# Two experts' weights loaded early into freed slots, four experts' weights behind the row fetch, and 22 extra products

## The chip, the cores and the metric

The kernel runs on one core of a Trainium2 chip. The core has TensorE (PE; matrix products), VectorE (DVE), ScalarE (ACT), GpSimd (POOL) and SyncE (SP), which here only issues transfers; 16 DMA engines move the data. The metric is the device time of one execution in microseconds; less is better.

## What is computed

An attention block (a recurrence with a decaying state, "RWKV-7") is followed by a mixture of experts that keeps at most 80 tokens for each expert:

```python
def _moe_ref(x, w_gate, w1, w2, capacity):
    logits = x @ w_gate                       # x: 3072 tokens x 320, 8 experts
    expert_idx = np.argmax(logits, axis=1)
    probs = softmax(logits)
    gate_w = probs[np.arange(N), expert_idx]
    out = np.zeros((N, D))
    for e in range(E):
        tok_idx = np.where(expert_idx == e)[0]
        if len(tok_idx) > capacity:           # 80: the largest gates stay
            gw = gate_w[tok_idx]
            tok_idx = tok_idx[np.argpartition(-gw, capacity)[:capacity]]
        h = np.maximum(x[tok_idx] @ w1[e], 0.0)          # 320 x 1024
        out[tok_idx] = gate_w[tok_idx, None] * (h @ w2[e])   # 1024 x 320
    return out
```

The attention has batch 4, 8 heads, 768 steps and head size 40; its output, one row of 320 for each of 3072 tokens, is x.

## The kernel before

The program has three parts.

**Part one, attention and gates.** 24 units (12 stretches of 64 steps, two pairs of batches) go through three nested helpers, `prepare`, `solve` and `finish`. The instructions aren't issued as written: each is handed with `add` to a planner (class `Plan`), with an engine, an estimated duration, the keys of the buffers that it reads and writes and a due time, and the planner writes out one list. Buffers are rings: `kb` (scaled k and b, ten slots of 4 KB per partition), `ah` (scaled a, ten slots of 2 KB) and `P` have a slot for each of the last ten units, `raww` two. All of them lie in the pool `hold`, which ends with part one. A unit's token rows go to the tensor `x_rows` in DRAM in batches (`rows_go`, L817; the last two batches are two units each). The gates are ranked as they come: `rank_early`, `rank_four`, `rank_late` and `rank_last` take the largest gates of each expert out in groups of eight (`extract`, L846 and L848, on VectorE) and merge sorted lists (`merge`, L853 and L865) into `tops[0]` and `tops[1]`. `rank_late` and `rank_last` use two `raww` slots, `pair_a` and `pair_b`, as scratch.

**Part two, the slots.** From `tops` comes a threshold for each expert (`thr`, `thw`, `thr_p`), then a 0/1 matrix `sel` of kept tokens (bf16, 128 x 384, called `selm` when flat), two products that count them (`tot` L1025, `pos` L1027), a scan, and the slot of each token. `hot` (three blocks of eight units, L1039) times `ids` gives `ids_p` (24 small products, L1042), and from it come the row numbers `idx_g` and `idx_s`. The order inside parts two and three is not written by hand: a scheduler of the framework sets it, engine by engine.

**Part three, the experts.** `load_expert` (L978 to L981) issues four transfers on SP for one expert: the first 256 rows of w1, the other 64 rows in two halves (`w1r`), and w2. All eight experts' weights have a place of their own in the pool `wpool`, which reuses the memory of `hold`, and all eight calls stand ahead of part two on SP. SP's transfers share eight completion semaphores, so that the ninth waits for the first. `gather(e)` (L1066, GpSimd) fetches the 80 rows of expert e from `x_rows` with an indirect DMA. `turn_x` transposes them (L1077, L1078) to `xe`; `first_layer` has 64 products with the 256 rows (L1092) and 32 with the rest (L1098); `second_layer` 80 products with w2 (L1111); `turn_y` transposes back, scales, and scatters the rows into the output (L1124, GpSimd).

## Time and profile before

| what | value |
|---|---|
| time, median of 3 runs | 559.41 us (554.07 to 560.3) |
| profiled execution | 556.64 us, of which the span is 554.9 us |
| PE busy in the span | 418.9 us (75%) |
| DVE busy | 311.2 us (56%) |
| POOL busy | 224.7 us (40%) |
| ACT busy | 182.0 us (33%) |
| moved by DMA | 73.06 MB, mean 132 GB/s |

The profile records one execution. Its span runs from the first to the last instruction; the profiled execution's own time is 1.7 us longer. Busy time is the sum of an engine's instructions; those that only issue a transfer or wait are not counted. A share of the whole span is a mean over three very different parts, so a table by stage is of more use here than the totals. [...]

### The profile page before, as it was taken

How to read it: one execution, taken by the hardware profiler on the slowest of the kernel's cores; microseconds unless marked ns; L12 is line 12 of the kernel's file. 1: busy time of each engine (PE TensorE's matmuls, PEld its weight loads, DVE VectorE, ACT ScalarE, POOL GpSimd, SP SyncE). 2: the span in 40 equal slices, each digit the busy share in tenths (PEclk: the TensorE clock that was granted, in tenths of full speed). 3: DMA queues.
4: the chain of work that ended last, by engine and by line, in shares of the span. 5: the costliest groups of instructions: out<-in, count | busy, mean ns of one | idle time of the engine just before them, and what ended most of it. 6: DMA issues, size and time to landing. Idle time of an engine off the chain costs nothing. (4 is left out here: it accounts for less than half of the span.)

```text
span 554.9 us, 24379 instructions
## 1 busy us (share of the span) xinstructions
PE 418.9 (75%) x10769; PEld 363.9 (66%) x10769; DVE 311.2 (56%) x706; ACT 182.0 (33%) x353; POOL 224.7 (40%) x395
## 2 busy tenths in 40 slices
PE   2754199797929988989898998999888102788795
PEld 2643078686818877878787887888777101677794
DVE  5868968536504745773577443966496995011121
ACT  2432063543522453444454443445223000110000
POOL 7010101888488410898599513883000002300111
PEclk9978569989866998988899799999699755688799
DMA  8775477576692677677577185314510009999900
GB/s 135 116 114 113 65 171 145 90 116 123 122 214 61 118 170 132 148 138 121 127 139 188 50 150 124 84 31 121 117 26 28 2 24 335 324 333 330 289 15 20
DMA packets 241453, 73.06 MB, mean 132 GB/s; under 512 B 217908, under 2 KB 235716, under 8 KB 241348
## 3 DMA queue, kind: packets, MB, share of 16 engines
q1 hardware_dynamic: 211428, 65.50, 52.3%
q10 hardware_dynamic: 29152, 4.36, 4.9%
q8 instruction: 85, 1.39, 1.0%
q0 software_dynamic: 768, 1.64, 1.0%
q14 instruction: 20, 0.16, 0.1%
HBM read 53.26 MB, written 18.13 MB: 129 GB/s over the span
## 5 line engine op out<-in xcount | busy, mean ns | idle before, releaser
L498 POOL TENSOR_TENSOR tmp<-lt 128x30 f32<-128x30 f32 (+9 forms) x150 | 86.1, 574 | 60.5 <-DMA lt<-blocks 49.7
L500 POOL TENSOR_TENSOR lt<-lt,tmp 128x30 f32<-128x30 f32 (+9 forms) x150 | 87.7, 585 | 11.8
L707 DVE TENSOR_TENSOR UL<-ps,mask 128x832 f32<-128x832 f32 x24 | 24.5, 1023 | 47.3 <-PE ps L702 47.3
L758 PE MATMUL ps<-wsel,xT 128*128 128x192 f32 x192 | 38.4, 344 | 2.3 <-DVE xT L748 1.4
L344 PE MATMUL ps<-ident,raww 128*128 128x128 f32 x88 | 17.5, 333 | 27.2 <-DMA raww<-in_w_dram 27.2
L344 PE MATMUL ps<-ident,kb 128*128 128x128 f32 x192 | 33.8, 304 | 4.8 <-DVE kb L407 3.5
L369 DVE TENSOR_TENSOR_SCAN P<-dec,begins 128x520 f32<-128x520 f32 x24 | 30.7, 1288 | 8.1 <-ACT dec L365 8.0
L485 POOL MEMSET nt<- 32x1024 f32 x12 | 11.4, 946 | 58.4 <-ACT nt L417 58.0
L758 PEld LDWEIGHTS ps<-wsel,xT 128*128 128x128 f32 x192 | 31.8, 196 | 4.4 <-DVE xT L748 1.7
L1124 POOL DMA_INDIRECT out_dram<-y,idx_s x8 | 7.4, 924 | 66.6 <-DVE y L1123 66.6
L735 DVE TENSOR_TENSOR st<-ps,st 128x832 f32<-128x832 f32 (+1 forms) x24 | 23.8, 991 | 18.6 <-PE ps L724 18.6
L377 DVE TENSOR_TENSOR_SCAN iv<-dec,ends 128x520 f32<-128x520 f32 x24 | 29.9, 1245 | 4.4 <-ACT ivc L396 3.7
L1111 PE MATMUL yp<-hT,w 128*64 128x80 f32 x640 | 29.6, 249 | 3.2 <-issue 3.0
L344 PEld LDWEIGHTS ps<-ident,raww 128*128 128x128 f32 x88 | 12.2, 169 | 28.8 <-DMA raww<-in_w_dram 22.8
L452 DVE TENSOR_TENSOR psi<-ps,mask 128x512 f32<-128x512 f32 x24 | 16.4, 688 | 25.4 <-PE ps L437 23.5
L407 DVE TENSOR_TENSOR kb<-rawkb,ps 128x640 f32<-128x640 f32 x22 | 17.9, 814 | 21.6 <-PE ps L344 13.2
L1111 PEld LDWEIGHTS yp<-hT,w 128*64 128x64 f32 x640 | 26.6, 148 | 5.0 <-issue 3.5
L344 PEld LDWEIGHTS ps<-ident,kb 128*128 128x128 f32 x192 | 23.7, 154 | 8.6 <-DVE kb L407 3.5
L611 ACT COPY rv<-ps 128x1024 f32<-128x1024 f32 x24 | 24.3, 1013 | 11.1 <-PE ps L344 7.2
L655 PE MATMUL ps<-VL,psi 64*64 64x104 f32 x768 | 27.2, 289 | 0.5 <-DVE VL L628 0.3
L1092 PE MATMUL hp<-xe,w 128*64 128x80 f32 x512 | 24.3, 259 | 2.8 <-issue 2.3
L1092 PEld LDWEIGHTS hp<-xe,w 128*64 128x64 f32 x512 | 23.1, 159 | 3.3 <-issue 2.4
(176 smaller groups left out, 953.7 us busy)
## 6 DMA issues: line engine op xcount, KB each, us to landing
w<-in_moe_w_dram SPq DMA_DIRECT2D x8, 1280.0 KB
w<-in_moe_w_dram SPq DMA_DIRECT2D x8, 1024.0 KB
VL<-in_v_dram SPq DMA_DIRECT2D x96, 40.0 KB, 2.3
out_dram<-zero SPq DMA_DIRECT2D x8, 480.0 KB
raww<-in_w_dram SPq DMA_DIRECT2D x44, 80.0 KB, 3.1
rawkb<-in_k_dram SPq DMA_DIRECT2D x44, 80.0 KB, 3.5
rawkb<-in_b_dram SPq DMA_DIRECT2D x44, 80.0 KB, 3.1
rawr<-in_r_dram ACTq DMA_DIRECT2D x84, 40.0 KB, 3.6
```

What stands on the lines that cost most here:

```text
L344: nc.tensor.matmul(o, lhsT=i, rhs=ident, start=True, stop=True, is_transpose=True, skip_group_check=True)
L369: nc.vector.tensor_tensor_scan(at("P", n), at("dec", n)[:, 0 : H * SEG], begins, 0.0, op0=Alu.mult, op1=Alu.add)
L377: nc.vector.tensor_tensor_scan(at("iv", n)[:, H * SEG : 0 : -1], at("dec", n)[:, H * SEG : 0 : -1], at("ends", n)[:, H * SEG : 0 : -1], 0. ...
L498: e.tensor_tensor(out=tv, in0=t3[:, 0:s, s : s + 1].to_broadcast([128, s, n]), in1=t3[:, s : s + 1, s + 1 :].to_broadcast([128, s, n]), op ...
L500: e.tensor_tensor(out=t3[:, 0:s, s + 1 :], in0=t3[:, 0:s, s + 1 :], in1=tv, op=Alu.add)
L611: nc.scalar.copy(at("rv", n).rearrange("p (k c) -> p k c", k=2), ps[:, bank(kr) : bank(kr) + 2, :])
L655: nc.tensor.matmul(ps[T * x : T * x + T, b0 + q, X * i : X * i + X], lhsT=psi[rows, q, i, :], rhs=at("VL", n)[rows, vo : vo + X], start=i ...
L707: nc.vector.tensor_tensor(out=view(at("UL", n), 0, (M4 * X, 2), (1, M4 * X)), in0=view(ps[:, bank(ku), :], 0, (512, 2), (1, M4 * X)), in1= ...
L735: nc.vector.tensor_tensor(out=view(st, o, (BS, M4), (step, 2), (1, n_)), in0=view(flat, 512 * bank(ky) + o, (4 * T, M4), (step, 2), (1, n_ ...
L758: nc.tensor.matmul(ps[:, b0, WS * m : WS * m + WX], lhsT=at("xT", n)[:, 2 * T * cof(m, 0) : 2 * T * cof(m, 0) + 2 * T], rhs=wsel_[:, WS * ...
L1092: nc.tensor.matmul(hp[j][c : c + 64, b // 2, :], lhsT=w1[:, i, FH * j + 64 * b : FH * j + 64 * b + 64], rhs=xe[:, i, :], start=i == 0 and ...
L1111: nc.tensor.matmul(yp[c : c + 64, b // 2, :], lhsT=w2[:, f, 64 * b : 64 * b + 64], rhs=hT[:, f, :], start=f == 0 and b < 2, stop=f >= (FK ...
```

## The change

**Early weights.** `early_weights(0)` and `early_weights(1)` are planned in part one. Each issues seven transfers on SP: w1 into two `kb` slots, w1's last 64 rows in two halves into an `ah` slot, and w2 in three pieces into three `kb` slots. Expert 0 takes the slots of units 14 to 18, expert 1 those of units 19 to 23. All ten `kb` slots, three `ah` slots and the scratch tiles `cd`, `la`, `lb` and `lc` move from `hold` to a pool `keep_` that stays until the end. `pair_a` and `pair_b` move from two `raww` slots to one of those `ah` slots.

**Later weights.** Only experts 2 to 7 have a place in `wpool`. Experts 2 and 3 are loaded where all were loaded; experts 4 to 7 are loaded behind `gather(0)` and a transfer of one word of its rows to DRAM (`word`) on SP, which waits for that gather to land.

**Products.** 22 products of `ones_b` with `selm` (bf16, 128 x 384) go into a PSUM tile `warm` that nothing reads.

```diff
+WARM = 22
...
+    KEPT = [("ah", NM - 10), ("ah", NM - 5), ("ah", NM - 8)] + [("kb", n) for n in range(LOOK)]
+    kept = {(n, i % LOOK): keep_.tile([128, COLS[n]], F32, name=f"{n}_{i % LOOK}") for n, i in KEPT}
...
-        buf = {n: [hold.tile([128, COLS[n]], F32, name=f"{n}_{i}") for i in range(RINGS[n])] for n in COLS}
+        buf = {n: [kept[n, i] if (n, i) in kept else hold.tile([128, COLS[n]], F32, name=f"{n}_{i}")
+                   for i in range(RINGS[n])] for n in COLS}
...
-        cd, la, lb, lc = (hold.tile([128, 128], F32, name=name) for name in ("cd", "la", "lb", "lc"))
+        cd, la, lb, lc = (keep_.tile([128, 128], F32, name=name) for name in ("cd", "la", "lb", "lc"))
...
-        pair_a, pair_b = at("raww", NM), at("raww", NM + 1)
+        pair_ = at("ah", NM - 8)
+        pair_a, pair_b = pair_[:, 0:256], pair_[:, 256:512]
...
+        def early_weights(e):
+            ks = range(NM - 10 + 5 * e, NM - 5 + 5 * e)
+            kbs = [at("kb", n) for n in ks]
+            rest = at("ah", ks[0])
+            w2s = [kbs[2 + i][:, 0 : DM * c].rearrange("p (c d) -> p c d", d=DM) for i, c in enumerate((3, 3, 2))]
+            weights[e] = kbs[0:2], rest, [w2s[f // 3][:, f % 3, :] for f in range(FK)]
+
+            def go():
+                for i in range(2):
+                    nc.sync.dma_start(kbs[i], moe_w1[e, 128 * i : 128 * i + 128, :])
+                for j in range(2):
+                    nc.sync.dma_start(rest[64 * j : 64 * j + 64], moe_w1[e, KW:, FH * j : FH * j + FH])
+                for i, o in enumerate(w2s):
+                    c = o.shape[1]
+                    nc.sync.dma_start(o, moe_w2[e, 384 * i : 384 * i + 128 * c, :].rearrange("(c p) d -> p c d", p=128))
+            add("SP", 4.5, 2.0, 0.0, go, [("tops", 0)],
+                [("kb", n) for n in ks] + [("ah", ks[0])], dma=7.5)
+
+        for e in range(2):
+            early_weights(e)
         rank_late()
         rank_last()
...
-    for e in range(E):
+    AHEAD = 4
+    for e in range(2, AHEAD):
         load_expert(e)
...
+        warm = ps_l.tile([128, NSEL], F32, name="warm")
+        for i in range(WARM):
+            nc.tensor.matmul(warm, lhsT=ones_b, rhs=selm, start=True, stop=True)
         row = sl.tile([cap, E], F32, name="row")
...
-    for e in range(E):
+    gather(0)
+    word = nc.dram_tensor("word", (1, 1), F32, kind="Internal")
+    nc.sync.dma_start(word[:, :], rows[0][0:1, 0:1])
+    for e in range(1, E):
         gather(e)
+    for e in range(AHEAD, E):
+        load_expert(e)
```

In part one the built order of every engine stays as it was, but for the early transfers on SP and the place of one merge of `rank_late` among the last VectorE rows. On SP, at the end of part one, there stands before (`lb<-la` is a merge's transfer, `w` and `w1r` are weights, one row for each call):

```order
L870 DMA lb<-la 8x128
L817 DMA x_rows<-xg_139 128x2x321 x2
L978 DMA w_0_6995<-in_moe_w_dram 128x2x1024
L980 DMA w1r_6996<-in_moe_w_dram 64x512 x2
L981 DMA w_0_6997<-in_moe_w_dram 128x8x320
L978 DMA w_1_7002<-in_moe_w_dram 128x2x1024
```

The two last writes of `x_rows` stand in a row there, and the weights of all experts follow. At the same place there stands now, with expert 0's weights in `kb` and `ah`:

```order
L879 DMA lb<-la 8x128
L824 DMA x_rows<-xg_142 128x2x321
L975 DMA kb_83<-in_moe_w_dram 128x1024
L975 DMA kb_84<-in_moe_w_dram 128x1024
L977 DMA ah_76<-in_moe_w_dram 64x512 x2
L980 DMA kb_85<-in_moe_w_dram 128x3x320
L980 DMA kb_86<-in_moe_w_dram 128x3x320
L980 DMA kb_87<-in_moe_w_dram 128x2x320
```

Expert 0's and expert 1's transfers went between the two writes of `x_rows`. Further on in SP's rows, from expert 1's last piece to expert 4's first:

```order
L980 DMA kb_82<-in_moe_w_dram 128x2x320
L824 DMA x_rows<-xg_142 128x2x321
L1004 DMA w_2_7012<-in_moe_w_dram 128x2x1024
L1006 DMA w1r_7013<-in_moe_w_dram 64x512 x2
L1007 DMA w_2_7014<-in_moe_w_dram 128x8x320
L1004 DMA w_3_7019<-in_moe_w_dram 128x2x1024
L1006 DMA w1r_7020<-in_moe_w_dram 64x512 x2
L1007 DMA w_3_7021<-in_moe_w_dram 128x8x320
L1160 DMA word<-rows 1x1
L1004 DMA w_4_7167<-in_moe_w_dram 128x2x1024
```

The last write of `x_rows` and experts 2 and 3 stand ahead of `word`, experts 4 to 7 behind it. On PE in part two there stands before:

```order
L1025 MATMUL tot<-sel,ones_b 128x384
L1027 LDWEIGHTS after_b
L1027 MATMUL pos<-sel,after_b 128x384
L1042 LDWEIGHTS hot
L1042 MATMUL ids_p<-ids,hot 80x24
```

There the products with `hot` follow `pos` at once. Now 13 of the 22 products stand between `pos` and the first product with `hot`, and three behind each eight of those; this is the end of the first eight and the first triple:

```order
L1069 LDWEIGHTS hot
L1069 MATMUL ids_p<-ids,hot 80x24
L1073 LDWEIGHTS ones_b
L1073 MATMUL warm<-sel,ones_b 128x384
L1073 LDWEIGHTS ones_b
L1073 MATMUL warm<-sel,ones_b 128x384
L1073 LDWEIGHTS ones_b
L1073 MATMUL warm<-sel,ones_b 128x384
L1069 LDWEIGHTS hot
L1069 MATMUL ids_p<-ids,hot 80x24
```

The scheduler spread the 22 products over part two; only the last three stand behind all the products that `idx_g` needs.

## Rows read from the trace of the kernel before

**Rows 1.** Busy time by stage: each engine, granted clock, DMA share, GB/s.

```profile
433.50:456.60 23.10, 0.61 (x3) 0.09 (x2) 21.88 (x98) 0.73 (x3) 0.56 (x3) 0.57 0.04 14
456.60:467.00 10.40, 3.16 (x27) 2.20 (x27) 7.85 (x17) 0.86 (x3) 0.90 (x4) 0.50 0.93 299
467.00:474.40 7.40, 0.00 (x0) 0.00 (x0) 0.00 (x0) 0.00 (x0) 5.38 (x8) 0.50 1.06 339
474.40:524.40 50.00, 41.93 (x859) 38.32 (x861) 8.51 (x20) 5.04 (x21) 5.41 (x6) 0.81 1.06 323
524.40:554.90 30.50, 23.71 (x609) 22.10 (x605) 5.61 (x12) 1.31 (x3) 4.58 (x5) 0.95 0.11 34
```

**Rows 2.** Timeline of SP's issues from 425 us: start, us, what.

```profile
428.05 17.90 SPq L817 DMA_DIRECT2D x_rows<-xg  x2
456.79 0.37 SPq L978 DMA_DIRECT2D w<-in_moe_w_dram  x1
```

**Rows 3.** Waits of SP's queue: total us, times, longest.

```profile
SPq L978 <- DVE tops L846: 8.3, 1, 8.3
```

**Rows 4.** Timeline, all engines, part two to the first layer of expert 0.

```profile
459.17 0.48 PE L1025 MATMUL tot<-sel,ones_b 128*128 128x384 bf16 x1 [0.99 <-DVE sel L1020]
459.44 0.53 PE L1027 MATMUL pos<-sel,after_b 128*128 128x384 bf16 x1
...
463.19 2.30 DVE L1039 TENSOR_TENSOR hot<-slot,iot 128x640 bf16<-128x640 f32 x3
...
464.07 2.18 PE L1042 MATMUL ids_p<-ids,hot 128*80 128x24 bf16 x24 [4.11 <-DVE hot L1039]
...
466.50 0.17 DVE L1046 TENSOR_SCALAR idx_g<-row 80x8 int32<-80x8 f32 x1
...
475.78 4.53 PE L1092 MATMUL hp<-xe,w 128*64 128x80 f32 x64 [0.50 <-DVE xe L1080]
...
480.25 1.27 PE L1098 MATMUL hp<-xe,w1r 64*64 64x80 f32 x32
```

**Rows 5.** Instructions on the tile rows: the gathers and all its transfers' landing.

```profile
L1066 POOL DMA_INDIRECT rows<-x_rows,idx_g x8: 906/910/1132, 468.0 to 476.7; - x8
...
DMA to landing us min/median/max: 6.4/6.9/8.0
```

**Rows 6.** Landing of the scatters into the output, from the tile view of out_dram.

```profile
DMA to landing us min/median/max: 2.4/3.0/7.1
```

**Rows 7.** Timeline of PE: the first products of experts 1 to 7's first layers.

```profile
482.54 0.28 PE L1092 MATMUL hp<-xe,w 128*64 128x80 f32 x1
...
488.32 0.23 PE L1092 MATMUL hp<-xe,w 128*64 128x80 f32 x1
...
499.42 0.23 PE L1092 MATMUL hp<-xe,w 128*64 128x80 f32 x1
...
511.32 2.43 PE L1092 MATMUL hp<-xe,w 128*64 128x80 f32 x64
...
524.42 0.34 PE L1092 MATMUL hp<-xe,w 128*64 128x80 f32 x1
...
532.84 0.23 PE L1092 MATMUL hp<-xe,w 128*64 128x80 f32 x1
...
540.30 0.23 PE L1092 MATMUL hp<-xe,w 128*64 128x80 f32 x1
...
542.74 0.78 PE L1098 MATMUL hp<-xe,w1r 64*64 64x80 f32 x32
```

**Rows 8.** PE alone in stretches of 1 us: busy, granted clock, DMA share, GB/s.

```profile
436.00:437.00 1.00, 0.00 (x0) 0.97 0.00 0
437.00:438.00 1.00, 0.00 (x0) 0.50 0.00 0
...
518.00:519.00 1.00, 0.00 (x0) 0.93 1.02 394
519.00:520.00 1.00, 0.38 (x7) 0.50 1.10 277
```

## The prediction

> **What bounds the kernel now.** I read the end of the program first, because everything the diff moves lies there. The table by stage [rows 1] cuts it into five. From 433.5 to 456.6 us VectorE alone works (21.88 of 23.10 us): it ranks the gates. The DMA engines are nearly free (share 0.04, 14 GB/s) and TensorE is busy for 0.61 us. From 456.6 to 467.0 the slots of the chosen tokens are worked out, a chain through VectorE and TensorE. From 467.0 to 474.4 no compute engine but GpSimd does anything: the rows of expert 0 are on their way. From 474.4 to 524.4 the DMA engines are full (1.06, 323 GB/s) and TensorE is busy for only 41.93 of 50.00 us. From 524.4 to the end TensorE sets the pace and the DMA share is 0.11.

> So the weights are the bound from 456.8 to about 525. SyncE issues the second-last write of x_rows at 428.05 and the last one 17.9 us later, and the first weight at 456.79 [rows 2]; before that weight it waited 8.3 us for VectorE's last MAX8 [rows 3], since the weight tiles take memory that the ranking still used. An expert has 320 x 1024 + 1024 x 320 words of 4 bytes, 2.62 MB; 8 of them are 21.0 MB, at 323 GB/s 65 us.

> What that costs TensorE is seen in the starts of the first layers for expert 0 and the others [rows 4, 7]: 475.78, 482.54, 488.32, 499.42, 511.32, 524.42, 532.84 and 540.30. The distances are 6.76, 5.78, 11.10, 11.90, 13.10, 8.42 and 7.46. The last has all weights present and no wait; the three of 11 to 13 are waits for weights.

> **The change part by part.**

> *Weights of experts 0 and 1.* Fourteen DMAs now stand on SP right behind the x_rows write of 428.05. The slots that they fill have no reader left after 433.5, when TensorE has three instructions in 23 us [rows 1]. 5.24 MB at 323 GB/s are 16.2 us, so they are done at about 446 to 450, in a stage where the DMA engines are free: cost nothing. Behind them on SP stands only the last x_rows write, issued at about 445.6 as before [rows 2] or up to 4 us later; it is needed by the fetch at 468.0 [rows 5], so it has some 15 us to spare. If that cover were gone, each us would be lost one for one.

> *Weights of experts 2 and 3.* The ranking's scratch moves into a slot that stays, so these no longer wait for the last MAX8 but for the last x_rows write, which I put at 449 (445.95 and about 3 us to land). 16.2 us more put their end at 465 to 468, before or just at the row fetch. Expert 2 is wanted some 20 us later.

> *Weights of experts 4 to 7 behind the row fetch.* SP waits for the first gather to land before it issues anything; queued behind it are only these 16 DMAs, and TensorE waits for them. They start at about 472 and need 10.5 MB / 323 GB/s = 32.5 us, to 505. By the starts worked out below expert 4 is wanted at 500 (its own weights land at about 481), expert 7 at 522. Cost nothing; the rate would have to fall under 10.5 MB / 50 us = 210 GB/s to matter, and the lowest full stage shows 299 [rows 1].

> *The row fetch.* A gather landed 6.4 us after its issue at the least while the weights ran [rows 5]. Scatters of as many rows landed in 7.1 at the most and 3.0 us in the median [rows 6], and five of the eight were issued after 524.4 [rows 1], when the weights had all but ended. With no weights on the engines I take 3.0: expert 0's rows at 471.0 instead of 474.4, **-3.4 us**. Bounds: 2.4, the least of the scatters (-4.0), and 6.4, nothing gained. [...]

> *TensorE without waits for weights.* From 475.78 to 540.30 are 64.52 us. With weights present I keep the first two distances (6.76 and 5.78, weights were there) and put 7.46 for the other five: 49.84. That is **-14.7 us**. The bound on the other side is 8.42, the other distance with its weights landed early in it, for all five: 54.64, so -9.9. I take 7.46, because it is the only one without a stretch at the lower clock. The part after the last start, 540.30 to 554.9, stays.

> *The 22 products.* In the built order they don't stand where the source has them: 13 come between pos and the first product for ids, three behind each group of eight. [...] I take **+0.8 us**, since which level holds there is open. Upper bound: 0.48 us each, the duration of tot, one after another: 13 end at 466.2, 2.1 late, and 6 more cost 2.9: +5.0. Lower bound: at the upper level the last eight products need only half their time behind the third hot (465.49), -0.4.

> *The clock at the first layer.* Expert 0's first layer took 475.78 to 481.52, 5.74 us, at the lower level; expert 7's took 540.30 to 543.52, 3.22 us [rows 4, 7]. If the products held the clock up until the rows land, 2.5 us would be saved. But the last products end at about 467 and the rows come at 471. In an idle stretch of the kernel before, from 433.5, the granted clock is 0.97 at 436 to 437 and 0.50 after; in a later one it is 0.93 at 518 to 519, with no product running, and 0.50 in the next [rows 8]. So I take **0**, with -2.5 as the bound.

> Sum: -3.4 - 14.7 + 0.8 = **-17.3 us**. The profiled execution took 556.64 us (span 554.9), so 539.3; it stands 2.8 us under the median of the three runs, 559.41, and on that median I forecast **542 us**.

> **The rivals.**

> *The clock stays up.* Then another 2.5 us are gained: 539.6. For it: the gap between the last product and the rows is only some 4 us. Against it: both idle stretches of rows 8 end at 0.50. [...]

> *The fetch is no shorter.* If its 6.4 us are its own and not the weights', term one goes and 545.5 is left. Against it: the scatters' 3.0.

> *The late weights bind.* Experts 4 to 7 start 15 us later than DMA engines allow. If the rate falls to 180 GB/s, expert 7 lands at 530 instead of the wanted 522: 550. No stage of rows 1 with full queues shows that.

> *The change doesn't take hold.* If the early DMAs were held until 456.8 as now, the first four experts would land at 491, the last four, behind the gather, at 525 as now, and the time would be 556 to 560. Against it: nothing between 428 and 456 in their slots is still read.

> *Slower.* TensorE becomes the only bound, so its clock decides. At the lower level a cycle is 5.74 / 3.22 = 1.78 times as long, so each us of the stage spent there costs 0.44 us; after 39 us of the some 64 the gain of 17.3 is spent, and with all of it the time is about 587. For it: in the stage 474.4 to 524.4 the mean granted clock is 0.81. Against it: that stage has idle stretches, and from 524.4 on, with none until the end, it is 0.95 [rows 1].

> **How the numbers follow.** Chances: the forecast 0.72, the clock stays up 0.10, the fetch no shorter 0.10, late weights 0.02, no hold 0.03, slower 0.03. Low end: 559.4 - 4.0 - 14.7 - 0.4 - 2.5 = 537.8, and since the runs of before reach 5.3 us below their median, 535. High end: with one term at its bad bound the time is 545.5 (fetch), 546.9 (cycles of 8.42) or 546.3 (products); with two of them up to 551. I set 549. A measurement of this kernel tells about 1% (5.6 us) from no change; the three runs spread by 1.1%. Faster by more than that are the first four, 0.94; within it the fifth, 0.03; slower 0.03.

> **What would show it.** In the changed profile: weights of experts 0 and 1 issued at 428 to 442 and a DMA share near 1 there; expert 2's first weight issued at about 449; the first gather landing about 3 us after issue; the first layer of expert 0 at 472 to 473; distances of about 7.5 us from expert 2 on and no wait of TensorE for weights; the first products for ids at 464 and the last at about 467; the clock at 0.50 when expert 0 starts. I'd be wrong if the distances stay at 8 us or more with weights present, if idx_g comes several us later, or if the stretch before 456 grows while 10 MB of weights are written beside the ranking.

## The result, and the profile after

The changed kernel took **540.48 us** in the median (538.6 to 543.25, 4 runs) and the kernel before 557.94 (554.07 to 560.3, 4 runs): a ratio of 0.970, 95% interval 0.962 to 0.977. The forecast was 542.0 us. The profiled execution took 539.98 us with a span of 538.2. The number was met; the way to it was not, as the rows show.

The table by stage of the changed kernel, with the stages of [rows 1] (columns: stretch, its length, busy time of PE, PEld, DVE, ACT and POOL, TensorE's granted clock as a share of full speed, DMA share, GB/s; in both kernels' traces the clock is at each moment 1.00 or 0.50, so a value between is a stretch with both):

```profile
428.00:450.90 22.90, 0.59 (x2) 0.09 (x2) 21.68 (x97) 1.40 (x6) 1.43 (x7) 0.57 0.93 291
450.90:460.90 10.00, 7.86 (x49) 4.24 (x49) 7.49 (x16) 0.00 (x0) 0.00 (x0) 0.61 0.98 327
460.90:465.40 4.50, 0.33 (x2) 0.20 (x2) 0.17 (x1) 0.39 (x2) 3.16 (x5) 1.00 0.14 37
465.40:501.60 36.20, 29.14 (x660) 27.07 (x661) 5.76 (x14) 3.81 (x17) 6.70 (x8) 0.86 1.03 311
501.60:538.20 36.60, 29.74 (x802) 28.24 (x801) 7.86 (x18) 2.02 (x6) 5.50 (x6) 0.99 0.09 25
```

The ranking, 23 us with a DMA share of 0.04 before, now has 0.93 beside it, and is no longer for that: the last MAX8 (VectorE's instruction that takes the eight largest values out, 0.41 us each) starts 9.1 us behind the first one of its ten, in both kernels. The row fetch (third row) runs on nearly free DMA engines (share 0.14). The stage with full queues is 36 us long instead of 50, but TensorE still stands idle for 7 of them.

SP's timeline and the tile of the gathered rows, as in [rows 2, 5]:

```profile
422.74 0.96 SPq L975 DMA_DIRECT2D kb<-in_moe_w_dram  x2
...
439.84 0.37 SPq L824 DMA_DIRECT2D x_rows<-xg  x1
443.56 0.37 SPq L1004 DMA_DIRECT2D w<-in_moe_w_dram  x1
...
465.06 0.27 SPq L1160 DMA_DIRECT2D word<-rows  x1
465.39 0.38 SPq L1004 DMA_DIRECT2D w<-in_moe_w_dram  x1
```

```profile
L1096 POOL DMA_INDIRECT rows<-x_rows,idx_g x8: 906/910/1132, 462.1 to 470.8; - x8
...
DMA to landing us min/median/max: 2.6/6.7/7.4
```

The first gather was issued at 462.1 and its rows are there at 465.0: 2.9 us instead of 6.4. The later seven run beside the weights again, hence the median of 6.7.

TensorE's timeline from expert 2 on, where [rows 7] had waits:

```profile
480.63 2.44 PE L1122 MATMUL hp<-xe,w 128*64 128x80 f32 x64 [1.37 <-issue]
...
484.41 1.05 PE L1141 MATMUL yp<-hT,kb 128*64 128x80 f32 x24
487.48 2.16 PE L1141 MATMUL yp<-hT,kb 128*64 128x80 f32 x56 [2.02 <-issue]
489.41 2.44 PE L1122 MATMUL hp<-xe,w 128*64 128x80 f32 x64
491.78 0.37 PE L1128 MATMUL hp<-xe,w1r 64*64 64x80 f32 x8
494.84 0.65 PE L1128 MATMUL hp<-xe,w1r 64*64 64x80 f32 x24 [2.69 <-issue]
...
496.12 4.63 PE L1141 MATMUL yp<-hT,w 128*64 128x80 f32 x80
500.58 0.72 PE L1122 MATMUL hp<-xe,w 128*64 128x80 f32 x15
502.93 1.27 PE L1122 MATMUL hp<-xe,w 128*64 128x80 f32 x31 [1.64 <-issue]
...
508.98 2.38 PE L1122 MATMUL hp<-xe,w 128*64 128x80 f32 x64
...
515.53 2.38 PE L1122 MATMUL hp<-xe,w 128*64 128x80 f32 x64
...
522.08 2.38 PE L1122 MATMUL hp<-xe,w 128*64 128x80 f32 x64
```

The first layers start at 466.35, 473.18, 480.63, 489.41, 500.58, 508.98, 515.53 and 522.08: distances of 6.83, 7.45, 8.78, 11.17, 8.40, 6.55 and 6.55. Look where the idle time stands: behind the 24th of 80 products with expert 1's w2, behind the 8th of 32 on w1r, behind the 15th of 64 on w1. A tile that the last product has just read can't be late. The view says "issue": nothing that it shows held TensorE. After the longest stall, of 2.69 us, the clock falls too: the granted clock is 0.50 from 497 to 499 (80 products from 496.12 in 4.63 us; the later 80 from 506.17, at 1.00, take 2.99).

From the start of the last MAX8 to the end of the span the time fell from 98.72 to 87.75 us: **11.0 us**, 3.7 of them ahead of expert 0's first layer and 7.3 behind it. The rest of the 16.7 us between the two profiled executions lies ahead of that MAX8 (456.18 and 450.45), where all engines have the same instructions in the same order, but for the early transfers on SP and one merge.

### The profile page after: what moved, and what is told of

It is laid out like the page before. It is cut to its first block, busy times and chain, and to the rows that moved or that the text cites. A ratio compares the mean times of both kernels' runs of the same rounds, so it can differ in the third digit from the quotient of the medians.

```text
span 538.2 us, 24437 instructions
## 1 busy us (share of the span) xinstructions
PE 404.7 (75%) x10791; PEld 349.4 (65%) x10791; DVE 312.0 (58%) x706; ACT 181.3 (34%) x353; POOL 225.1 (42%) x395
## 5 line engine op out<-in xcount | busy, mean ns | idle before, releaser
L505 POOL TENSOR_TENSOR tmp<-lt 128x30 f32<-128x30 f32 (+9 forms) x150 | 84.3, 562 | 64.3 <-DMA lt<-blocks 53.6
L507 POOL TENSOR_TENSOR lt<-lt,tmp 128x30 f32<-128x30 f32 (+9 forms) x150 | 89.1, 594 | 11.8
L765 PE MATMUL ps<-wsel,xT 128*128 128x192 f32 x192 | 39.6, 353 | 2.3 <-DVE xT L755 1.4
L351 PE MATMUL ps<-ident,kb 128*128 128x128 f32 x192 | 32.1, 293 | 4.3 <-DVE kb L414 2.0
L351 PEld LDWEIGHTS ps<-ident,raww 128*128 128x128 f32 x88 | 11.5, 162 | 28.7 <-DMA raww<-in_w_dram 16.2
L414 DVE TENSOR_TENSOR kb<-rawkb,ps 128x640 f32<-128x640 f32 x22 | 17.9, 813 | 17.4 <-PE ps L351 11.6
L351 PEld LDWEIGHTS ps<-ident,kb 128*128 128x128 f32 x192 | 22.4, 148 | 8.0 <-issue 4.0
L709 PE MATMUL ps<-W,nt 64*64 64x104 f32 x768 | 24.0, 261 | 1.9 <-DVE cd L847 1.7
L696 ACT COPY W<-ps 128x832 f32<-128x832 f32 x24 | 20.5, 855 | 13.6 <-PE ps L691 7.4
L662 PE MATMUL ps<-VL,psi 64*64 64x104 f32 x768 | 24.3, 265 | 0.8 <-DVE VL L635 0.4
L731 PE MATMUL ps<-UL,kb 64*64 64x104 f32 (+1 forms) x768 | 23.1, 261 | 2.1 <-DVE UL L714 2.1
L202 POOL TENSOR_SCALAR_AFFINE_SELECT lt<-lt 128x1024 f32<-128x1024 f32 x6 | 9.3, 1544 | 34.2 <-DVE lt L507 33.8
## 6 DMA issues: line engine op xcount, KB each, us to landing
w<-in_moe_w_dram SPq DMA_DIRECT2D x6, 1280.0 KB, 13.8
```

The source lines that it names most:

```text
L351: nc.tensor.matmul(o, lhsT=i, rhs=ident, start=True, stop=True, is_transpose=True, skip_group_check=True)
L505: e.tensor_tensor(out=tv, in0=t3[:, 0:s, s : s + 1].to_broadcast([128, s, n]), in1=t3[:, s : s + 1, s + 1 :].to_broadcast([128, s, n]), op ...
L507: e.tensor_tensor(out=t3[:, 0:s, s + 1 :], in0=t3[:, 0:s, s + 1 :], in1=tv, op=Alu.add)
L662: nc.tensor.matmul(ps[T * x : T * x + T, b0 + q, X * i : X * i + X], lhsT=psi[rows, q, i, :], rhs=at("VL", n)[rows, vo : vo + X], start=i ...
L709: nc.tensor.matmul(ps[T * bb : T * bb + T, b0 + q, X * i : X * i + X], lhsT=tm[rows, q, i, :], rhs=at("W", n)[rows, wo : wo + X], start=Tr ...
L731: nc.tensor.matmul(ps[HB * q : HB * q + HB, b0 + bb, yo + lo : yo + hi], lhsT=at("kb", n)[rows, o : o + HB], rhs=at(name, n)[rows, vo + lo ...
```

## The experiments

**The theory.** While weights fill the DMA queues, TensorE's own instructions, which come by DMA as well (the DMA view of either kernel has 85 packets of the kind "instruction" on one queue), arrive late; each of its stalls is the end of one block of instructions. **The rivals:** the stalls are waits for weights after all, or belong to the products' own chain through VectorE and ScalarE. Beside it: is the part ahead of the last MAX8 changed, or was it chance?

All runs in one table, from their profiles (us). "The hold" is that the weights of experts 4 to 7 wait for the first gather. In unread, not_loaded and twice part of the output comes from other weights; they are there for their times alone. The column "both" is the sum of the two before it; ratios are to the kernel before on the same chip, with 95% intervals.

| run | last MAX8 starts | from it to expert 0's first layer | from there to the end | both | median | ratio |
|---|---|---|---|---|---|---|
| before | 456.18 | 19.60 | 79.12 | 98.72 | 557.94 | |
| after | 450.45 | 15.90 | 71.85 | 87.75 | 540.48 | 0.970 (0.962 to 0.977) |
| no_products | 452.91 | 15.87 | 71.42 | 87.29 | 542.03 | 0.981 (0.975 to 0.988) |
| no_hold | 454.14 | 19.20 | 66.16 | 85.36 | 542.94 | 0.985 (0.978 to 0.991) |
| unread | 449.63 | 15.81 | 71.96 | 87.77 | 540.60 | 0.983 (0.976 to 0.990) |
| not_loaded | 451.42 | 15.91 | 60.27 | 76.18 | 531.21 | 0.965 (0.959 to 0.971) |
| after_again | 445.64 | 15.72 | 71.84 | 87.56 | 539.50 | 0.980 (0.972 to 0.989) |
| before_again | 454.96 | 20.01 | 81.33 | 101.34 | 558.04 (one run) | |
| before_hold | 451.72 | 20.10 | 79.18 | 99.28 | 553.37 | 1.002 (0.999 to 1.005) |
| e01_late | 443.40 | 20.68 | 71.12 | 91.80 | 542.31 | 0.986 (0.981 to 0.991) |
| twice | 455.40 | 15.76 | 84.64 | 100.40 | 558.01 | 1.005 (1.000 to 1.010) |
| products_on | 455.66 | 18.59 | 71.25 | 89.84 | 545.99 | 0.980 (0.972 to 0.988) |
| flow | 460.02 | 19.05 | 67.23 | 86.28 | 552.45 | 0.996 (0.991 to 1.000) |
| flow_on | 461.06 | 18.23 | 69.21 | 87.44 | 553.43 | 1.000 (0.996 to 1.005) |

The kernel before had 552.70 us on the chip of no_products to not_loaded, 551.46 on that of after_again to e01_late, 555.02 on that of the last four.

### unread: weights that nobody reads

```diff
         weights[e] = [w1[:, i, :] for i in range(2)], w1r, ...
+        if e >= 4:
+            weights[e] = weights[2 + e % 2]
```

> The changed kernel, in which experts 4 to 7 are loaded as before but their products read the weights of experts 2 and 3 (part of the output is another one). The DMA traffic is the same, only no product can wait for a weight that comes after 465. My theory: TensorE's stalls of 1.4 to 2.9 us in mid group (479.26 to 480.63, 485.46 to 487.48, 492.15 to 494.84, 501.3 to 502.93) are its own instruction fetches, held up by the weights that fill the DMA engines; then they stay, distances of the first layers stay near 6.8, 7.5, 8.8, 11.2, 8.4, 6.6, 6.6, and the time at 540.5, within 2. Rival, waits for late weights: the stalls go, all distances from expert 3 on near 6.6, 7 us faster: 533.

The stalls stay, at the same products and nearly to the hundredth as long as in the changed kernel:

```profile
479.71 2.43 PE L1124 MATMUL hp<-xe,w 128*64 128x80 f32 x64 [1.38 <-issue]
...
486.57 2.16 PE L1143 MATMUL yp<-hT,kb 128*64 128x80 f32 x56 [2.02 <-issue]
...
493.93 0.65 PE L1130 MATMUL hp<-xe,w1r 64*64 64x80 f32 x24 [2.69 <-issue]
...
501.98 1.88 PE L1124 MATMUL hp<-xe,w 128*64 128x80 f32 x48 [1.63 <-issue]
```

No product can have waited for a weight issued behind the fetch, those of experts 0 to 3 were there by then (in the changed kernel the DMA share is 0.05 from 460 to 464), and 87.77 us against 87.75 say that no product of the changed kernel waited for a weight either. The first rival is out.

### not_loaded: no weights behind the fetch

```diff
     for e in range(AHEAD, E):
-        load_expert(e)
+        weights[e] = weights[2 + e % 2]
```

> The changed kernel in which the weights of experts 4 to 7 are not loaded at all and their products read those of experts 2 and 3 (part of the output is another one). After the row fetch there is no DMA traffic but rows. My theory (instruction fetches held up by weights): the instruction packets come every 4 to 5 us from 465 on instead of every 7 to 8, no stalls of over 1 us in mid group, distances near 6.6 from the second on, and the time 6 to 9 us lower, 532 to 535. Rival, late weights: the same gain here, but then also in the run that loads the weights and doesn't read them. Rival, the stalls belong to the products' own chain (PSUM, VectorE, ScalarE): distances stay at 8.8 and 11.2, no gain, 540.

All waits of TensorE from 464 us to the end that remain:

```profile
PE xp L1107 <- DMA rows<-x_rows,idx_g: 4.2, 1, 4.2
PE yq L1150 <- DVE yT L1144: 0.5, 1, 0.5
PE hp L1122 <- DVE xe L1110: 0.5, 1, 0.5
PE yp L1141 <- ACT hT L1131: 0.2, 1, 0.2
```

"issue" is gone, the distances are 5.47, 5.78, 6.67 and four times 6.55, and the time is 9.4 us under that of unread on the same chip (11.6 by the profiles). The chain of the products takes 6.55 us per expert; the second rival is out. Eight gathers on free queues landed in 2.5 to 2.8 us.

The instruction packets of the DMA view (packets, MB, share), in the changed kernel from 465 to 503 and from 503 to 536 us:

```profile
q8 instruction: 5, 0.08, 0.9%
...
q8 instruction: 7, 0.11, 1.6%
```

and in not_loaded from 466 to 521 us:

```profile
q8 instruction: 12, 0.20, 1.6%
```

A packet is 16 KB (16,384 bytes in the trace), and the whole program has 85 of them. TensorE has 10,791 products and as many weight loads, 21,582 instructions or 254 for each packet, and from one stall to the next stand just so many (counted under twice). So by their number the packets are TensorE's; some 64 bytes for an instruction are an estimate from these counts. Without weights one comes every 4.6 to 4.7 us (55 / 12, 33 / 7), beside weights every 7.6 us (38 / 5). 4.6 us is no limit of the DMA engines: 183 products in 6.55 us make 128 in 4.6, TensorE's own pace.

The trace has each packet's time too. Set beside the stalls, that of the kernel before included:

```profile
491.57 3.19 PE L1092 MATMUL hp<-xe,w 128*64 128x80 f32 x42 [2.25 <-issue]
...
498.26 1.39 PE L1111 MATMUL yp<-hT,w 128*64 128x80 f32 x33 [0.16 <-issue]
...
504.67 0.35 PE L1098 MATMUL hp<-xe,w1r 64*64 64x80 f32 x3 [2.04 <-issue]
...
519.62 1.60 PE L1111 MATMUL yp<-hT,w 128*64 128x80 f32 x19 [2.85 <-issue]
```

| kernel | a 16 KB packet has landed at | TensorE goes on at |
|---|---|---|
| before | 490.07, 496.91, 503.25, 518.15 | 491.57, 498.26, 504.67, 519.62 |
| after | 479.05, 486.14, 493.49, 501.47 | 480.63, 487.48, 494.84, 502.93 |

In both kernels each of these stalls ends 1.3 to 1.6 us behind such a landing. A packet's own transfer takes 0.9 to 1.6 us in them, with weights (1.1 to 1.3 in the changed kernel from 465 to 503) and without (0.9 to 1.4 behind that). What differs is when it starts: in the changed kernel 4.4 to 5.5 us behind a restart of TensorE while weights flow (480.63 to 485.04, 494.84 to 500.33), and behind them, where nothing stops for a packet, 0.0 to 1.2 us behind a block's first product (502.93 to 504.10, 530.65 to 530.76; blocks of 127 counted from 502.93). So the packets wait behind the weights, and TensorE for the packets.

### twice: more of the traffic

Products as in unread, and behind the weights of experts 4 to 7 the same 16 DMAs once more into the same tiles.

```diff
     for e in range(AHEAD, E):
         load_expert(e)
+    for e, w1, w1r, w2 in again:
+        nc.sync.dma_start(w1, ...)   # and w1r twice, w2, as in load_expert
```

> The changed kernel, in which experts 4 to 7 use the weights of experts 2 and 3 (part of the output is another one) and the weights of experts 4 to 7 are written twice over into their own tiles, unread. 10.5 MB more, so the DMA engines stay full until some 534 us instead of 501. My theory (instruction fetches held up by traffic): the stalls go on to the end, one each 127 products, 1.3 to 2.9 us each: three or four more, with the lower clock behind them 2 to 4.5 us per expert for three experts, +8 to +12 us beside the changed kernel: about 550; the distances of experts 5, 6 and 7, 8.4, 6.6 and 6.6 before, become 9 to 12. The stalls up to expert 4 stand at the same products as in the changed kernel. Rival (stalls belong to the first experts or to their weights): no change, 540.

Nine stalls instead of four; beside the first four, at the old places, these:

```profile
515.53 1.60 PE L1146 MATMUL yp<-hT,w 128*64 128x80 f32 x40 [3.11 <-issue]
...
522.84 0.37 PE L1133 MATMUL hp<-xe,w1r 64*64 64x80 f32 x8 [2.92 <-issue]
...
529.97 1.33 PE L1127 MATMUL hp<-xe,w 128*64 128x80 f32 x32 [0.39 <-issue]
...
536.38 0.98 PE L1146 MATMUL yp<-hT,w 128*64 128x80 f32 x22 [1.51 <-issue]
...
543.14 3.33 PE L1146 MATMUL yp<-hT,w 128*64 128x80 f32 x89 [1.96 <-issue]
```

The last three distances become 11.74, 11.33 and 8.89, and the time behind the last MAX8 grows by 12.65 us, just over the 8 to 12 expected: traffic that no instruction needs takes back the whole gain of the change. From one restart of TensorE to the next are 6.4 to 8.1 us here and 6.9 to 8.1 in the changed kernel, whatever the products between them do. Count these: from expert 2's first product on w1 to the 25th on its w2 stand 64 + 32 + 3 + 4 + 24 = 127 products, each with a weight load, so 254 instructions; 16 KB over these are some 64 bytes each. From restart to restart stand 126 to 128 products in each run that has stalls, or 254, twice that, where a block's end passed without one (before, before_hold).

### no_products: the stalls move with the program

```diff
-WARM = 22
+WARM = 0
```

> The changed kernel without its 22 products of no use. My theory: they buy and cost nothing. The granted clock was 1.00 at 458 to 464 in the changed kernel's profile, but 0.50 again from 466, when expert 0's rows are there, and ids came no later than before. So the time should be that of the changed kernel, 540.5 us, within 1.5. Rival, the products hold the clock for expert 0's first layer: 2.5 us slower, 543. Rival, they delay idx_g (upper bound of the prediction): up to 5 us faster, 536. In the profile: first layer of expert 0 at the lower level in any case, its start 15.9 us behind the last MAX8's start, within 0.5.

No difference: 87.29 us from the last MAX8 to the end, and the first gather is issued 11.6 us behind that MAX8 in both. But look at the counts of what is left of each group behind a stall:

```profile
483.91 1.68 PE L1121 MATMUL hp<-xe,w 128*64 128x80 f32 x42 [2.11 <-issue]
...
490.74 1.34 PE L1140 MATMUL yp<-hT,kb 128*64 128x80 f32 x33 [1.92 <-issue]
...
497.69 0.35 PE L1127 MATMUL hp<-xe,w1r 64*64 64x80 f32 x2 [2.63 <-issue]
...
505.50 1.19 PE L1121 MATMUL hp<-xe,w 128*64 128x80 f32 x27 [0.88 <-issue]
```

64 - 42 = 22 products into expert 2's w1 instead of 0, 47 into its w2 instead of 24, 30 into w1r instead of 8, 37 into expert 4's w1 instead of 15: each stall stands 22 products further on, as many as were taken out of the stream far ahead of it (one count is 23). So a stall belongs to an address in the program, not to a tile. This had not been expected in the text above; the next runs have it among their expectations.

### products_on: 16 more products, until the rows land

```diff
+        row_b = sl.tile([cap, 128], BF16, name="row_b")
+        nc.scalar.copy(row_b..., row.unsqueeze(2).to_broadcast([cap, E, 16]))
+        for i in range(TAIL):   # TAIL = 16
+            nc.tensor.matmul(warm, lhsT=row_b, rhs=selm[0:cap], start=True, stop=True)
```

> The changed kernel with 16 more products of no use, which wait for the ids and so run until expert 0's rows land. If they hold the granted clock at 1.00, expert 0's first layer takes 3.2 to 3.5 us instead of 5.9, and the time falls by 2.5 us, to 538. If the clock falls all the same, no change. And the stalls: the instruction stream is longer by 16 products and their loads, so by my theory each stall moves 16 products up: expert 2's on w2 from the 25th product to the 9th, expert 3's from the 9th of w1r's 32 to about the 57th of w1's 64. Rival (stalls belong to a weight tile or a buffer): they stay at the same products.

The stalls moved up by 16, as the theory has it (8 into expert 2's w2, 56 into expert 3's w1). The clock stays untested: GpSimd's copy ahead of the first gather now waited for the last of these products, so the rows came 2.7 us later and TensorE was idle for 4.1 us again. No gain is seen: the ratio is 0.980, that of the changed kernel in after_again.

```profile
469.09 0.23 POOL L1096 COPY pair<-ident 64x64 f32<-64x64 f32 x1 [19.24 <-PE warm L1081]
...
508.21 3.94 PE L1127 MATMUL hp<-xe,w 128*64 128x80 f32 x64 [2.69 <-DMA w<-in_moe_w_dram]
```

The second row warns of a name. By it expert 4's first product waits for its weight. That DMA was issued at 454.80, 53 us earlier, and the DMA share was down to 0.24 from 468 to 470, so it had landed; but the fourth stall, 16 products up from the 16th product on this tile, must fall within one product of here, and a 16 KB packet landed at 506.8, 1.4 us earlier. So the 2.69 us that stand there under the weight's name are by the times of that DMA and of the packet another wait for instructions.

### no_hold: weights of all experts ahead of the fetch

```diff
-    AHEAD = 4
+    AHEAD = 8
...
-    word = nc.dram_tensor("word", (1, 1), F32, kind="Internal")
-    nc.sync.dma_start(word[:, :], rows[0][0:1, 0:1])
```

> The changed kernel with the weights of experts 4 to 7 issued right behind those of 2 and 3 instead of behind the first gather's landing. My theory has two halves. The gather runs under full queues again: 6.4 us or so from issue to landing instead of 2.9, +3.5 us to the first layer of expert 0. On the other side the weights end some 15 us earlier (10.5 MB from about 450 instead of 465), so TensorE's stalls in mid group end earlier too (distances of expert 2 to 4 fall from 8.8, 11.2 and 8.4 to nearer 7), which gives back 2 to 4 us. Sum: within 2 us of the changed kernel, 539 to 542. Rival, the stalls are waits for weights: then loading them earlier takes all of the stalls away, -6 us, and +3.5 for the fetch: 538. Rival, the gather is no slower: 535 to 538.

As the first half says, the gathers land in 6.2 us at the least, +3.3 us to the first layer; as the second, the stalls are shorter and one fewer, -5.7 us behind it. Net -2.4 us by the profile, and no difference in the medians (542.94 against 540.60 for unread, intervals of the ratios overlapping). So the hold gives the fetch what it takes from the layers, or by the profile a little less: it is a matter of when the 21 MB flow.

### after_again and before_again: the part ahead of the last MAX8

The two kernels unchanged.

> The changed kernel once more, on another chip. In its first profile the last MAX8 of the ranking started at 450.45 us, in that of the kernel before at 456.18, though no instruction ahead of it stands in another order. From that MAX8 to the end are 87.75 us against 98.72: 11.0 us. My theory: the 5.7 us ahead of it are chance, and the change is worth 11.0 us, a ratio of 0.980 to the kernel before. Rival, the change also shortens the part ahead: 17 us, a ratio of 0.970. In either case the stalls should stand at the same products: at the first of expert 2's 64 products on w1, the 25th of its 80 on w2, the 9th of expert 3's 32 on w1r.

> The kernel before, one look on the same chip as the others of this group. If the 5.7 us ahead of the last MAX8 are chance, its MAX8 starts here within 3 us of the changed kernel's; if they belong to the change, again some 5 to 6 us behind it. From the MAX8 to the end 98.7 us, within 1.5. TensorE's stalls at expert 2's 23rd product on w1 and expert 3's 30th on w1r, as in the first profile, 22 products behind those of the changed kernel, since the instruction stream is shorter by 22 products and their loads.

0.980 is the first theory's ratio. The two profiles don't show it by themselves: their last MAX8 start 9.3 us apart, further than in the first pair, and neither expectation of 3 or of 5 to 6 us holds. But the changed kernel's profiled run was its shortest (535.0 us; the median is 539.50). 0.980 (0.972 to 0.989) of 551.46 us is a gain of 10.9 us (6 to 16), and 11.0 to 13.8 lie behind the MAX8 by the two pairs of profiles, so about nothing is left for the part ahead; a few us either way stay possible. unread and no_products, which are the changed kernel up to there, say the same on another chip (0.983 and 0.981). From the MAX8 to the end the kernel before took 101.34 us, outside the 98.7 within 1.5 that were expected: its waits for "issue" are 12.5 us in all here and 7.3 in the first profile. The stalls of the changed kernel stand at the products named, and so do those of the kernel before, 42 and 3 products from a group's end:

```profile
491.52 1.74 PE L1092 MATMUL hp<-xe,w 128*64 128x80 f32 x42 [2.66 <-issue]
...
504.50 0.35 PE L1098 MATMUL hp<-xe,w1r 64*64 64x80 f32 x3 [1.76 <-issue]
```

### before_hold: the hold alone

The kernel before with `word` behind the first gather and experts 4 to 7 loaded behind it.

```diff
-    for e in range(E):
+    for e in range(4):
         load_expert(e)
...
```

> The kernel before with only the hold of the change: weights of experts 4 to 7 issued behind the first gather's landing; those of experts 0 to 3 stay behind the last MAX8, at 457. The first four experts' 10.5 MB take 32 us from 457, so they still run when the gather is issued at 468: it lands in 6.4 us as before. The last four then start at about 474 while the first four still run, behind them on the queue: nothing moves. My theory: no change, within 2 us of the kernel before, and stalls of TensorE at the same products. Rival, the hold itself shortens the fetch: 3.4 us faster. Rival, weights of experts 4 to 7 come late and products wait: slower by 3 us or more.

As expected: 1.002, gathers from 6.3 us on, 99.28 us, the stalls at the same products. The hold is worth nothing while the first four experts' weights are still on their way at the fetch.

### e01_late: the early weights late

```diff
-        for e in range(2):
-            early_weights(e)
         rank_late()
         rank_last()
+        add("SP", ..., lambda: nc.sync.dma_start(late_word[:, :], tops[1][0:1, capr - 1 : capr]), ...)
+        for e in range(2):
+            early_weights(e)
```

> The changed kernel with the weights of experts 0 and 1 issued only when the last MAX8 has its result, some 27 us later than in the changed kernel, on the same slots; the hold and the products stay. My theory: the gather runs under full queues again (6.4 us for 2.9: +3.5 us to expert 0's first layer), and the traffic lasts until some 520 instead of 501, so that two or three more of TensorE's instruction fetches come late, 1.5 to 3 us each and as much again at the lower clock: distances of 8 to 11 us up to expert 6. Sum +8 to +11 us: about 550 where the changed kernel has 540.5, nearly all of the change's gain. Rival, the early weights matter only by the row fetch: +3.5, 544. Rival, they bring nothing (the gain is the hold's): 540.5.

4.1 us by the profile (542.31 beside 539.50 by the medians, the intervals of the ratios overlapping), not 8 to 11: the expectation missed what SP would do with the time. It issued the weights of expert 2 and the first of expert 3 meanwhile, from 432.33 on, so the DMA share from 430 to 450 is 0.81 all the same, and full queues lie beside the layers for 37 us, about as in the changed kernel (35). So it came out as its first rival has it, and what the run shows is the fetch alone: 6.1 us and more to land, expert 0's first layer 4.8 us later, and nothing lost behind that (71.12 us).

### flow and flow_on: can both be had?

```diff
+    LATE = [("xg", 0), ("lgp", 0), ("lgp", 1), ("lg", 0), ("gsm", 0)]   # these, first and tok in keep_
...
-                nc.sync.dma_start(x_dram[...], xg)
+                (nc.scalar if bi == 6 else nc.sync).dma_start(x_dram[...], xg)
...
-    AHEAD = 4
+    AHEAD = 5
```

flow_on is this with the 16 products of products_on.

> The changed kernel with the last write of x_rows on ScalarE's queue, the buffers that it and the last gates use in slots that stay, and expert 4's weights ahead of the hold: SP then issues five experts' weights in a row from 423 on, instead of waiting for x_rows behind the second. The gather is issued at 462 on free or nearly free queues, and behind the hold three experts are left, 7.9 MB: traffic ends at about 490 instead of 501. By my theory one or two stalls fewer: distances of experts 3 to 5 fall from 11.2 and 8.4 to nearer 7 and 6.6, 3 to 5 us faster from the last MAX8 to the end (87.7), about 537. Rival: the five experts still run when the gather is issued, then it lands 3.5 us later and the gain is gone.

> Both of the last two: weights of five experts in a row, and 16 more products until the rows land. If both theories hold, their gains add: 5 to 7 us faster than the changed kernel, about 534, and from the last MAX8 to the end 81 to 83 us against 87.7.

Both miss. Of flow's two halves the stalls became shorter (67.23 us), but the fifth expert's weights still ran at the fetch, as its rival said: 1.5 us in all. And the part ahead of the MAX8, with no instruction moved but that one write and a few beside it on GpSimd and ScalarE, became some 5 to 10 us longer (460 and 461 beside 455.4 and 455.7 on the same chip; by the medians 464 beside 454 to 456). By the profiles all of it is there before the early weights start: SP issues the write of x_rows just ahead of them at 431.88 in flow and at 422.29 in the changed kernel. The buffers lie at other addresses; that this costs the time, and how, is not shown. No version with the full output beats the changed kernel by more than can be measured.

## Why the prediction was right, and where it was not

- **What bounds the kernel: wrong.** The prediction said that the weights were the bound and that the distances of 11 to 13 us were waits for weights. In the changed kernel they aren't (unread). In the kernel before they aren't either: its stalls end 1.4 to 1.5 us behind the landing of an instruction packet, as shown, and its weights were there. SP's ninth transfer of weights waits for its first (the first eight were issued from 456.79 to 461.32, the ninth held SP for 4.87 us from 461.97 on), and an expert has four, so w2 of experts 2 to 5 had landed when w2 of experts 4 to 7 went out:

```profile
487.76 0.59 SPq L981 DMA_DIRECT2D w<-in_moe_w_dram  x1
...
495.58 1.70 SPq L981 DMA_DIRECT2D w<-in_moe_w_dram  x1
...
504.45 0.59 SPq L981 DMA_DIRECT2D w<-in_moe_w_dram  x1
...
512.25 0.59 SPq L981 DMA_DIRECT2D w<-in_moe_w_dram  x1
```

  The first layers of experts 2 to 5 began at 488.32, 499.42, 511.32 and 524.42. The prediction's own 323 GB/s from 456.8 on puts these weights at 481, 489, 497 and 505; it did not set them beside the starts.
- **TensorE without waits for weights, -14.7 us: the step that failed.** From expert 0's first layer to the end the gain was 7.3 us (9.5 by the second pair of profiles). No wait for weights ended, as there was none; there is less traffic beside the layers. That time goes with the length of the traffic: with 0, 24, 35 and 67 us of full DMA engines behind expert 0's start it is 60.27 (not_loaded), 66.16 (no_hold), 71.85 (after) and 84.64 us (twice); the kernel before, in its other order, has 49 and 79.12. How the gain divides is not settled: in the first pair the waits for "issue" didn't shrink (7.3 us before, 7.7 after) and the lower clock lasted some 10 us instead of 19 (0.86 of 36.20 us, 0.81 of 50.00), in the second pair they fell from 12.5 to 7.9. The weights of experts 4 to 7, costed at nothing because they are in time, cost 9.4 to 11.6 us (not_loaded): by holding up instructions, and by the lower clock behind the stalls. 1.4 of the 11.6 lie in expert 0's distance (6.83 and 5.47), where no stall is.
- **The 7.46 us as the cycle** was misread too. In that stretch stand 104 products of second layers, not 80: the order of the kernel before draws parts of the second layers forward. The true cycle is 6.55 us, and the order after the change leaves 1.5 us more behind the last first layer (16.1 instead of 14.6), which the prediction had put at nothing.
- **The row fetch, -3.4: right.** 6.4 to 2.9 us; first layer 3.7 earlier. Eight gathers on free queues took 2.5 to 2.8 us (not_loaded), close to the 3.0 that the forecast took from the scatters.
- **The 22 products, +0.8: nothing.** No run shows the 0.8 us: from the last MAX8 to the end are 87.75 us with the products and 87.29 without (no_products). 13 stand in the gap for hot, as said; idx_g starts 10.19 us behind the last MAX8 (10.32 before), with the granted clock up when the two triples ran (0.85 from 458 to 460, then 1.00).
- **The clock at the first layer, 0: right.** Rows of the changed kernel, as in [rows 8]; the seventh number is the granted clock:

```profile
460.00:462.00 2.00, 0.90 (x12) 0.44 (x10) 0.62 (x5) 0.00 (x0) 0.47 (x2) 1.00 0.05 16
462.00:464.00 2.00, 0.00 (x0) 0.00 (x0) 0.00 (x0) 0.00 (x0) 1.60 (x2) 1.00 0.05 13
464.00:466.00 2.00, 0.73 (x3) 0.38 (x3) 0.11 (x1) 0.39 (x2) 1.39 (x3) 0.86 0.32 90
466.00:468.00 2.00, 1.65 (x24) 1.65 (x26) 0.30 (x1) 0.39 (x2) 1.70 (x2) 0.50 0.72 166
```

  The products raised it to 1.00 (without them it is 0.50 through all of that stretch, in no_products), and 4 us without one lost it just when the rows came; expert 0's first layer took 5.8 us (5.7 before). TensorE waited 4.2 us for the rows, and the clock was 0.50 from 466 on.
- **Early weights of experts 0 to 3 at nothing: right.** They ran beside the ranking (DMA share 0.93) without lengthening it (9.1 us from the first to the last of its ten MAX8, as before).
- **The sum.** -17.3 us were forecast and -17.5 measured. Of these some 11 to 14 are the change's, by the profiles and by the second comparison (0.980), and the rest, 4 to 6 us ahead of the last MAX8, fell to the first comparison by chance, as far as the runs show. The range held; the agreement to 1.5 us is luck, since the largest term came out at half its size.

## What to carry to other kernels

A wait between two instructions that read the same tile is not a wait for that tile: before an idle stretch is priced as late data, look at which product of a group it stands ahead of, and whether it moves when instructions far ahead of it are taken out. Bulk transfers beside a stream of many short products were not free here though their data was early: they cost 9.4 to 11.6 us (not_loaded), since the instructions of each block of 127 products had to come through the same full DMA engines. So load early, into stretches where TensorE has little to do, and count a transfer's cost by how long it runs beside such a stream, as well as by when its data is wanted.
